# Re-timing the gates, input terms and early loads of a fused recurrence and feed-forward kernel

## The chip, the cores and the metric

The kernel runs on one core of one Trainium2 chip. The metric is device time in microseconds (us); lower is better. Kernels are compared only within the same rounds.

## The reference, cut to what matters

```python
# x, f_logit: (4, 6080, 256); lower_bound: (256,); w_in: (256, 2048); w_out: (2048, 256)
sig = 1 / (1 + exp(-f_logit))
f = lower_bound + (1 - lower_bound) * sig
for t in range(S):                       # a linear recurrence along the tokens
    h = f[:, t] * h + (1 - f[:, t]) * x[:, t]
    y[:, t] = h
h = y.reshape(24320, 256) @ w_in         # "first matmul"
out = (h * cos(h)) @ w_out               # "second matmul"
```

## The kernel before

Tokens go in chunks: seven of 256 (0 to 6), then chunks of 512 from chunk 7 on. For each chunk:

- a *gate* (tanh on ScalarE), *less-one* (tanh − 1), then the *terms* ih and u = (tanh − 1)·x;
- a transposition (by TensorE for chunks 0 to 3, by DMA later), the *forget gate* ff (GpSimd from chunk 4), two *scans* ya (VectorE, one for each half of the 256 features), and two *casts* yb to fp16 (GpSimd from chunk 4);
- then groups of the first matmul, a cosine (ScalarE), a product T (VectorE), and the second matmul.

The first matmul of a chunk needs both casts. In the traces here an engine takes its instructions in the order in which the program emits them, so the program weaves the preparation of later chunks between the groups of the current one. "(s, g)" is the place after group g of chunk s; "step s" is the stretch in which TensorE runs chunk s's first matmul.

```python
NPE, NSMALL = 4, 7
...
def less_one(c):                                   # ScalarE
    nc.scalar.activation(ig[:, ks, :], ig[:, ks, :], AFT.Identity, bias=-1.0, scale=1.0)

def pool_term(c):                                  # GpSimd: ih, then u
    nc.gpsimd.tensor_copy(by_half(ih), split(ig))
    for k in range(nt):
        nc.gpsimd.tensor_tensor(by_half(u)[:, k], split(ig)[:, k], split(xt)[:, k], AOP.mult)
...
def cast(c, i, a=0, b=None):
    ...
    eng = nc.vector if c < NPE else nc.gpsimd
    eng.tensor_scalar(yb[:, a:b], held[f"ya{i}", c][:, a:b], hc[:, i:i + 1], None, AOP.mult)
...
def front(c):
    gate(c); less_one(c); pool_term(c); turn(c)

FRONT = {NPE: (NPE - 2, 0), 5: (3, 0), 6: (3, 2), NSMALL: (4, 0), NSMALL + 1: (5, 0)}
for c in range(3, NC):
    ...
    elif c < NSMALL:
        at(c - 1, 0, forget(c)); at(c - 1, 0, recur(c, 0), cast(c, 0))
        at(c - 1, 1, recur(c, 1), cast(c, 1))
    elif c == NSMALL:
        at(c - 2, 3, forget(c))
        ...                                        # recur and cast as above
    if c >= NPE:
        if c in FRONT:
            at(*FRONT[c], front(c))
        else:
            at(c - 3, groups(c - 3) - 1, gate(c))
            at(c - 2, 0, less_one(c), pool_term(c), turn(c))
...
for s in range(2, NC):
    emit_load(s + 4)
    for g in range(groups(s)):
        moe1(s, g)                                 # first matmul, cosine, product
        moe2(*steps.pop(0))                        # a piece of the second matmul of chunk s - 1
        for what in weave.get((s, g), []):
            what()
```

(The `at` calls are shown without their lambdas.)

## Time and profile before

| | |
|---|---|
| time before | 694.66 us, median of 3 (693.38 to 694.71) |
| TensorE busy | 674.7 us of a span of 693.3 |
| TensorE idle before 90 us | 15.5 us |
| from the bulk start of chunk 8 (85.66 us) to the end | 607.6 us |

How to read it: TensorE is the engine that sets the time, so only its idle time and its clock matter. From 90 to 650 us it never pauses. What counts is at what moment the *bulk* of each early chunk's first matmul starts. One of its matmuls can begin with the first cast alone (a row "x1"); the rest, the bulk, needs the second. In the timeline the bulk is the row "x7" (chunks of 256) or "x3" (chunks of 512) that shows the wait; where there is no such wait, it is the row of the whole group, "x8" or "x4". The lines are in the prediction.

### The profile page before, as it was taken

Reading aid. Unit: us, or ns where it says so; the run is one execution under the profiler, and the core shown is the slowest. Engines: PE = TensorE matmul, PEld = TensorE weight load, DVE = VectorE, ACT = ScalarE, POOL = GpSimd, SP = SyncE. Lnnn points to the kernel's source line nnn. Section 1 sums busy time; section 2 is a strip of 40 time slices with the busy share of each in tenths; the row PEclk is TensorE's granted clock in tenths of the full one; section 3 lists DMA queues with packets and bytes.
Section 4 is the critical chain, followed back from the end, with each engine's and each line's share of the span. In section 5 each row is a group of like instructions: output and inputs, shape, how many; then the busy total and the mean of one; then the engine's idle time right before and its main releaser. Section 6 shows DMA issues by size and latency. Waiting matters only on the chain.

```text
span 693.3 us, 12206 instructions
## 1 busy us (share of the span) xinstructions
PE 674.7 (97%) x4726; PEld 484.8 (70%) x4726; DVE 583.9 (84%) x511; ACT 521.7 (75%) x593; POOL 390.8 (56%) x440
## 2 busy tenths in 40 slices
PE   6988899999999999999999999999999999999998
PEld 4787577777777777777777777777777777777776
DVE  5776878888888888888888888888888888888884
ACT  6685777778777877787778777877787778777763
POOL 3366656565656565656565656565556555655510
PEclk9999999999999999999999999999999999999999
DMA  9568557756864676468557765576457746662401
GB/s 230 157 179 209 144 126 180 145 122 164 177 147 122 161 183 142 122 156 187 145 122 156 185 146 122 158 184 146 122 154 180 153 122 153 184 151 62 92 31 61
DMA packets 172138, 101.99 MB, mean 147 GB/s; under 512 B 99120, under 2 KB 170544, under 8 KB 172080
## 3 DMA queue, kind: packets, MB, share of 16 engines
q1 hardware_dynamic: 170048, 97.54, 58.3%
q0 software_dynamic: 1760, 3.67, 2.2%
q8 instruction: 37, 0.61, 0.4%
q14 instruction: 21, 0.17, 0.1%
q10 hardware_dynamic: 272, 0.00, 0.0%
HBM read 54.00 MB, written 24.90 MB: 114 GB/s over the span
## 4 chain that ended last, share of the span: by engine, by line
PE 88%; DVE 3%; POOL 3%; ACT 2%; issue 2%; DMA 1%; SPq 0%; POOLq 0%; ACTq 0%
PE pb L286 44%; PE pa L250 44%; DVE T L265 2%; DMA xt<-in_x_dram 1%; DVE ya L214 1%; POOL u L158 1%; POOL yb L225 1%; ACT cs L259 1%; ACT ig L145 1%; POOL ih L156 0%; ACT ig L122 0%; SPq L82 0%; DVE u L138 0%; DVE yb L225 0%; ACT yb L221 0%
## 5 line engine op out<-in xcount | busy, mean ns | idle before, releaser
L265 DVE TENSOR_TENSOR T<-pa,cs 128x1024 f16<-128x1024 f32 x380 | 449.7, 1212 | 94.3 <-ACT cs L259 94.1
L259 ACT ACTIVATE cs<-pa 128x1024 f32<-128x1024 f32 x380 | 388.5, 1026 | 153.8 <-PE pa L250 149.2
L250 PE MATMUL pa<-yb,wi 128*128 128x512 f16 (+2 forms) x1640 | 393.2, 366 | 12.8 <-POOL yb L225 7.1
L286 PE MATMUL pb<-wo,T 128*128 128x256 f16 x3040 | 393.4, 273 | 0.0
L286 PEld LDWEIGHTS <-T 128*128 128x128 f16 x3040 | 297.7, 98 | 103.8 <-DVE T L265 0.3
L250 PEld LDWEIGHTS <-wi 128*128 128x128 f16 x1640 | 183.3, 114 | 94.1 <-issue 13.1
L225 POOL TENSOR_SCALAR yb<-ya,hc 128x512 f16<-128x512 f32 (+1 forms) x94 | 143.3, 1525 | 152.9 <-DVE ya L214 147.2
L214 DVE TENSOR_TENSOR_SCAN ya<-ff,ya,ut 128x512 f32<-128x512 f32 (+4 forms) x94 | 130.6, 1389 | 0.0
L158 POOL TENSOR_TENSOR u<-ig,xt 128x256 f16<-128x256 f32 x182 | 128.5, 739 | 0.0
L156 POOL CAST ih<-ig 128x1024 f16<-128x1024 f32 (+1 forms) x47 | 47.7, 1016 | 110.1 <-ACT ig L145 110.1
L195 POOL TENSOR_SCALAR ff<-it,hp 128x512 f32<-128x512 f16 (+1 forms) x94 | 63.0, 684 | 1.4 <-DMA it<-ih 1.4
L294 ACT COPY osb<-pb 128x512 f32<-128x512 f32 x93 | 53.9, 579 | 0.0
L122 ACT ACTIVATE ig<-zt 128x1024 f32<-128x1024 f32 (+2 forms) x52 | 51.5, 991 | 1.0 <-DMA zt<-in_f_logit_dram 0.9
L145 ACT ACTIVATE ig<-ig 128x1024 f32<-128x1024 f32 (+1 forms) x47 | 48.8, 1038 | 0.2
L310 PE MATMUL warm<-junk 128*128 128x512 f16 x14 | 6.0, 585 | 1.3 <-POOL junk L302 1.3
L138 DVE SCALAR_TENSOR_TENSOR u<-ig,xt 128x512 f16<-128x512 f32 (+1 forms) x5 | 2.9, 582 | 3.2 <-DMA xt<-in_x_dram 3.2
L214 DVE TENSOR_TENSOR_SCAN ya<-ff,ut 128x320 f32<-128x320 f32 (+2 forms) x6 | 5.6, 927 | 0.0
L214 DVE TENSOR_TENSOR_SCAN ya<-ff,ya,tp 128x256 f32<-128x256 f32 (+1 forms) x8 | 5.0, 665 | 0.6 <-ACT ff L192 0.4
L291 DVE COPY osb<-pb 128x256 f32<-128x256 f32 x4 | 1.7, 425 | 4.5 <-PE pb L286 4.5
L336 POOL COPY mark<-wo 128x1 f16<-128x1 f16 x1 | 0.2, 188 | 8.9 <-DMA wo<-in_moe_w_out_dram 8.9
L192 ACT ACTIVATE ff<-tp,hc 128x256 f32<-128x256 f16 (+1 forms) x10 | 3.7, 424 | 1.7 <-PE tp L172 1.6
L221 ACT ACTIVATE yb<-ya,hc 128x256 f16<-128x256 f32 (+1 forms) x5 | 2.3, 465 | 3.2 <-DVE ya L214 3.2
(27 smaller groups left out, 28.3 us busy)
## 6 DMA issues: line engine op xcount, KB each, us to landing
zt<-in_f_logit_dram SPq DMA_DIRECT2D x44, 512.0 KB, 5.1
xt<-in_x_dram SPq DMA_DIRECT2D x44, 512.0 KB, 6.2
out_dram<-osb SPq DMA_DIRECT2D x43, 512.0 KB, 3.4
out_dram<-osb SPq DMA_DIRECT2D x7, 256.0 KB, 2.6
wir<-in_moe_w_in_dram SPq DMA_DIRECT2D x2, 512.0 KB, 5.5
wo<-in_moe_w_out_dram POOLq DMA_DIRECT2D x4, 256.0 KB, 8.5
zt<-in_f_logit_dram POOLq DMA_DIRECT2D x4, 256.0 KB, 3.6
xt<-in_x_dram POOLq DMA_DIRECT2D x4, 256.0 KB, 3.7
```

Source lines behind the costliest of these rows:

```text
L122: nc.scalar.activation(ig[:, ks, :], zt[:, ks, :], AFT.Tanh, bias=0.0, scale=0.5)
L145: nc.scalar.activation(ig[:, ks, :], ig[:, ks, :], AFT.Identity, bias=-1.0, scale=1.0)
L156: nc.gpsimd.tensor_copy(by_half(ih), split(ig))
L158: nc.gpsimd.tensor_tensor(by_half(u)[:, k], split(ig)[:, k], split(xt)[:, k], AOP.mult)
L195: nc.gpsimd.tensor_scalar(f[:, a:b], igt[:, i, 0:b - a], hp[:, i:i + 1], 1.0, AOP.mult, AOP.add)
L214: nc.vector.tensor_tensor_scan(ya[:, p:q], f[:, p:q], ut[:, i, p - a:q - a], init, AOP.mult, AOP.add)
L225: eng.tensor_scalar(yb[:, a:b], held[f"ya{i}", c][:, a:b], hc[:, i:i + 1], None, AOP.mult)
L250: nc.tensor.matmul(pa[c, g][:, jq, a:b], win_block(i, jt), held[f"yb{i}", c][:, a:b], start=(i == 0), stop=(i == ND - 1))
L259: nc.scalar.activation(cs[c, g], pa[c, g], AFT.Sin, bias=float(_HALF_PI), scale=1.0)
L265: nc.vector.tensor_tensor(T, pa[c, g], cs[c, g], AOP.mult)
L286: nc.tensor.matmul(ps[:, ts % 2, :], Tt[c, jt][:, ts * P:(ts + 1) * P], wo[:, jt, :], start=(jt == 0), stop=(jt == NJ - 1))
L294: nc.scalar.copy(osb[:, ts - 1:ts + 1, :], ps)
```

## The change

Its intent: the gates and terms of each chunk are issued a step sooner, the early token loads move from GpSimd's to SyncE's queue, chunk 0's second matmul is woven with chunk 1's first, and chunks 2 and 3 get their terms from ScalarE and GpSimd instead of VectorE. No matmul is added or removed. The core of the diff (the bookkeeping of layouts for chunks 2 and 3, and lambdas rewritten as `later(...)`, are cut):

```diff
 def less_one(c):
-        nc.scalar.activation(ig[:, ks, :], ig[:, ks, :], AFT.Identity, bias=-1.0,
-                             scale=1.0)
+        if NPE <= c < NSMALL:
+            nc.gpsimd.tensor_scalar(ig[:, ks, :], ig[:, ks, :], -1.0, None, AOP.add)
+        else:
+            nc.scalar.activation(ig[:, ks, :], ig[:, ks, :], AFT.Identity, bias=-1.0,
+                                 scale=1.0)
 ...
-    load_wout(3)
-
-    mark2 = cpool.tile([P, 1], f16, name="mark2")
-    nc.gpsimd.tensor_copy(mark2, wo[:, NJ - 1, 0:1])
-    emit_load(3, q=nc.gpsimd)
+    w_in_place = load_wout(3)
+
+    for c in range(3, 7):
+        for k in emit_load(c):
+            if c == 3:
+                tc.add_manual_dep(k.ins, w_in_place.ins.name, ...)
 ...
+    gate(2)
+    less_one(2)
+    pool_term(2)
     moe1(1, 0)
-    moe1(1, 1)
-    gate(2)
-    term(2)
-    moe1(1, 2)
-    moe1(1, 3)
     moe2(0, 0)
+    mm1(1, 1)
+    cosine(1, 1)
+    moe2(0, 1)
     turn(2)
     forget(2)
     settle(2)
-    for h in range(1, 4):
-        moe2(0, h)
+    product(1, 1)
+    moe1(1, 2)
+    moe2(0, 2)
+    moe1(1, 3)
+    moe2(0, 3)
+    gate(3)
+    less_one(3)
+    pool_term(3)
 ...
-    FRONT = {NPE: (NPE - 2, 0), 5: (3, 0), 6: (3, 2), NSMALL: (4, 0), NSMALL + 1: (5, 0)}
+    FRONT = {NPE: ((2, 0), (2, 0)), NPE + 1: ((2, 2), (2, 3))}
 ...
+        if c == NPE:
+            f, slots = (c - 1, 1), ((c - 1, 1), (c - 1, 2))
 ...
+        first, second = FRONT.get(c, ((c - 3, groups(c - 3) - 1), (c - 2, 0)))
+        at(*first, later(gate, c))
+        at(*second, later(less_one, c), later(pool_term, c), later(turn, c))
 ...
-    for c in range(4, 6):
-        emit_load(c, q=nc.gpsimd)
-        if s + 4 < NC:
-            emit_load(s + 4)
+        if s + 5 < NC:
+            emit_load(s + 5)
```

More of the change, by code (lines that the diff above doesn't have):

```diff
@@ L105, in load_wout @@
     def load_wout(q):
-        nc.gpsimd.dma_start(
+        return nc.gpsimd.dma_start(
             wo[:, q * wc:(q + 1) * wc, :],
@@ L122, in gate @@
         nc.scalar.activation(ig[:, ks, :], zt[:, ks, :], AFT.Tanh, bias=0.0, scale=0.5)
-        if c >= NPE:
-            return
         if c == 0:
@@ L152, in pool_term @@
         u = hold("u", c, [P, CH // P, D], f16, 3)
-        by_half = lambda t: (t.rearrange("p k d -> p (k d)")[:, 0:nt * D]
-                             .rearrange("p (i k d) -> p k i d", i=ND, k=nt))
         split = lambda t: t[:, 0:nt, :].rearrange("p k (i d) -> p k i d", i=ND)
+        if c < NPE:
+            by_half = split
+        else:
+            by_half = lambda t: (t.rearrange("p k d -> p (k d)")[:, 0:nt * D]
+                                 .rearrange("p (i k d) -> p k i d", i=ND, k=nt))
         nc.gpsimd.tensor_copy(by_half(ih), split(ig))
@@ L163, in turn @@
         if c < NPE:
-            if c < 3:
-                d = ppool.tile([P, 2, ND, HALF], f16, tag="p2", bufs=2, name=f"tp{c}_{a}")
-            else:
-                d = ppool.tile([P, 2, ND, HALF], f16, tag="p1", bufs=3, name=f"tp{c}",
-                               padded_shape=[P, 2, ND, CH])
+            d = ppool.tile([P, 2, ND, HALF], f16, tag="p2", bufs=2, name=f"tp{c}_{a}")
             for q, src in enumerate((held["ih", c], held["u", c])):
@@ L192, in forget @@
                 nc.scalar.activation(f[:, a:b], igt[:, i, 0:b - a], AFT.Identity,
-                                     bias=1.0, scale=hc[:, i:i + 1])
+                                     bias=1.0, scale=(hc if c < 2 else hp)[:, i:i + 1])
             else:
@@ L332 @@
     load_wout(2)
-    load_wout(3)
-    mark2 = cpool.tile([P, 1], f16, name="mark2")
-    nc.gpsimd.tensor_copy(mark2, wo[:, NJ - 1, 0:1])
-    emit_load(3, q=nc.gpsimd)
+    w_in_place = load_wout(3)
+    for c in range(3, 7):
+        for k in emit_load(c):
+            if c == 3:
+                tc.add_manual_dep(k.ins, w_in_place.ins.name, mybir.DependencyInfo(
+                    mybir.DependencyClass.Sync, mybir.DependencyReason.DATA))
     keep_warm(7)
@@ L382, with later @@
     settle(2)
-    for h in range(1, 4):
-        moe2(0, h)
-    def front(c):
-        gate(c)
-        less_one(c)
-        pool_term(c)
-        turn(c)
+    product(1, 1)
[6 more added lines that the diff above has]
+    pool_term(3)
     weave = {}
-    FRONT = {NPE: (NPE - 2, 0), 5: (3, 0), 6: (3, 2), NSMALL: (4, 0), NSMALL + 1: (5, 0)}
+    FRONT = {NPE: ((2, 0), (2, 0)), NPE + 1: ((2, 2), (2, 3))}
     def at(s, g, *what):
         weave.setdefault((s, g), []).extend(what)
+    def later(f, *args):
+        return lambda: f(*args)
@@ L400 @@
     for c in range(3, NC):
         if c < NPE:
-            at(c - 1, 0, lambda c=c: gate(c), lambda c=c: term(c))
-            at(c - 1, 1, lambda c=c: turn(c), lambda c=c: forget(c), lambda c=c: settle(c))
+            at(c - 1, 1, later(turn, c), later(forget, c), later(settle, c))
+            continue
+        if c == NPE:
+            f, slots = (c - 1, 1), ((c - 1, 1), (c - 1, 2))
         elif c < NSMALL:
-            at(c - 1, 0, lambda c=c: forget(c))
-            at(c - 1, 0, lambda c=c: recur(c, 0), lambda c=c: cast(c, 0))
@@ L407 @@
-            at(c - 1, 1, lambda c=c: recur(c, 1), lambda c=c: cast(c, 1))
+            f, slots = (c - 1, 0), ((c - 1, 0), (c - 1, 1))
         elif c == NSMALL:
-            at(c - 2, 3, lambda c=c: forget(c))
-            at(c - 1, 0, lambda c=c: recur(c, 0), lambda c=c: cast(c, 0))
-            at(c - 1, 1, lambda c=c: recur(c, 1), lambda c=c: cast(c, 1))
-        else:
-            at(c - 1, 0, lambda c=c: forget(c))
-            at(c - 1, 2, lambda c=c: recur(c, 0), lambda c=c: cast(c, 0))
-            at(c - 1, 4, lambda c=c: recur(c, 1), lambda c=c: cast(c, 1))
@@ L416 @@
-        if c >= NPE:
-            if c in FRONT:
-                s, g = FRONT[c]
-                at(s, g, lambda c=c: front(c))
-            else:
-                at(c - 3, groups(c - 3) - 1, lambda c=c: gate(c))
-                at(c - 2, 0, lambda c=c: less_one(c), lambda c=c: pool_term(c),
-                   lambda c=c: turn(c))
+            f, slots = (c - 2, 3), ((c - 1, 0), (c - 1, 1))
+        else:
+            f, slots = (c - 1, 0), ((c - 1, 2), (c - 1, 4))
+        at(*f, later(forget, c))
@@ L425 @@
+        for i, slot in enumerate(slots):
+            at(*slot, later(recur, c, i), later(cast, c, i))
+        first, second = FRONT.get(c, ((c - 3, groups(c - 3) - 1), (c - 2, 0)))
+        at(*first, later(gate, c))
+        at(*second, later(less_one, c), later(pool_term, c), later(turn, c))
     steps = [(c, h) for c in range(1, NC) for h in range(2 * chunks[c][1] // P)]
-    for c in range(4, 6):
-        emit_load(c, q=nc.gpsimd)
     for s in range(2, NC):
-        if s + 4 < NC:
-            emit_load(s + 4)
+        if s + 5 < NC:
+            emit_load(s + 5)
```

## The prediction

> **What bounds the kernel now.** I read the page first (busy shares, slices), then the busy table by stretch, then the waits of TensorE, then the timelines of TensorE and GpSimd over the first 90 us. The page and the busy table:
>
> ```profile
> PE 674.7 (97%) x4726; PEld 484.8 (70%) x4726; DVE 583.9 (84%) x511; ACT 521.7 (75%) x593; POOL 390.8 (56%) x440
> ```
> ```profile
> 50.00:60.00 10.00, 7.09 (x50) 5.69 (x49) 5.88 (x7) 5.56 (x6) 6.80 (x10) 0.83 1.15 276
> ...
> 90.00:100.00 10.00, 10.00 (x72) 7.12 (x70) 9.09 (x9) 6.92 (x8) 6.80 (x8) 1.00 0.39 54
> ...
> 300.00:400.00 100.00, 100.00 (x695) 71.00 (x694) 87.65 (x75) 78.12 (x87) 59.41 (x66) 1.00 0.68 154
> ```
>
> Columns after the stretch are its length, busy us of PE, PEld, DVE, ACT, POOL, then granted clock. From 90 to 650 us TensorE never stops, at full clock, and the change neither adds nor removes a matmul. So 600 of the 693 us can't move. The movable part is before 90 us: summing length less PE busy over its nine stretches gives 15.5 us idle (2.3 of it before any data exists), plus stretches at a granted clock of 0.5. The waits of TensorE name two causes:
>
> ```profile
> PE pa L250 <- POOL yb L225: 7.1, 5, 2.9
> PE pa L250 <- DVE T L265: 4.0, 3, 2.2
> ```
>
> The five waits for yb are one at the start of each of chunks 4 to 8. The longest, chunk 5, in TensorE's and then GpSimd's timeline (start, length):
>
> ```profile
> 50.80 0.27 PE L250 MATMUL pa<-yb,wi 128*128 128x256 f16 x1
> 53.99 0.92 PE L250 MATMUL pa<-yb,wi 128*128 128x256 f16 x7 [2.91 <-POOL yb L225]
> 54.75 1.85 PE L286 MATMUL pb<-wo,T 128*128 128x256 f16 x8
> ```
> ```profile
> 48.00 0.93 POOL L225 TENSOR_SCALAR yb<-ya,hc 128x256 f16<-128x256 f32 x1 [1.26 <-ACT ig L145]
> 48.87 1.04 POOL L156 CAST ih<-ig 128x1024 f16<-128x1024 f32 x1
> 49.88 3.15 POOL L158 TENSOR_TENSOR u<-ig,xt 128x256 f16<-128x256 f32 x4
> 53.02 0.92 POOL L225 TENSOR_SCALAR yb<-ya,hc 128x256 f16<-128x256 f32 x1
> ...
> 68.74 1.57 POOL L225 TENSOR_SCALAR yb<-ya,hc 128x512 f16<-128x512 f32 x1 [3.32 <-DVE ya L214]
> 71.05 1.56 POOL L225 TENSOR_SCALAR yb<-ya,hc 128x512 f16<-128x512 f32 x1 [0.74 <-DVE ya L214]
> ```
>
> GpSimd casts the first half of chunk 5's scan, then works 4.2 us on a later chunk's cast and input term (ih, u of chunk 7), and only then casts the second half, whose scan had ended at 51.15. TensorE has one matmul to do and waits. After it, eight matmuls take 1.85 us instead of 1.04: half clock. The last two lines are chunk 7: nothing stands between its two casts, and TensorE waits only 1.28 us.
>
> **What the Trainium skill says.** "Perfetto Trace Analysis", section on the tensor engine instruction: VectorE, ScalarE and GpSimd take instructions strictly in order. The trace agrees: the cast ready at 51.15 starts at 53.02, when u ends. So the order of GpSimd's queue decides, not its 56% share. "TensorE: Matmul & The Clock Gate", Part 1: an idle window of about 3.4 us (free-running) halves the clock, and a busy window restores it. Here the clock is 0.50 from about 17.4 to 20.7 us and 54.9 to 58.3 us, each after an idle of 2.2 and 2.9 us; both begin on one grid of 3.41 us (11 windows apart). Each costs about 1.7 us. Idles of 1.3 us brought none. "GPSIMD Engine Reference", 3.1: about 2.6 cycles an element for two inputs, 512 elements of one input at best 769 ns. Here u of 256 elements takes 739 ns, the forget gate of 512 697 ns, but the yb cast of 512 1566 ns: dearer than the page's best.
>
> **The change part by part.**
>
> *Early loads on SyncE.* Six load issues of GpSimd (0.73 us each, 4.4 us at 19.84 to 24.27) and an 8.9 us wait for w_out leave its queue. GpSimd did nothing useful then (next work at 31.10), and no load wait of consequence stands in the first 90 us behind chunk 1. Worth 0 by itself; it makes room for chunk 2's and 3's terms.
>
> *Chunks 2 and 3.* Their ih and u leave VectorE (0.42 + 0.68 us each), which is the limit from 12.3 to 27 us, and go to ScalarE (0.63) and GpSimd (0.6 + 1.4). Chunk 0's second matmul is woven with chunk 1's first. The 2.19 us wait at 16.84 and the dip after it stay, since everything before is unchanged. From there TensorE has, until chunk 2's first matmul, 8 groups of 0.87 us, 0.7 of transposes and 1.7 of dip: 26.2 at the earliest, against 26.80 (bulk 27.29). Chunk 3's start comes out at about 34.1 against 35.31. Gain 1.1 us.
>
> *Chunk 4.* Its two scans move one group later (behind products 1 and 2 of chunk 3 instead of 0 and 1). Group 2's matmul begins 3.5 us into the step, its product ends about 3.5 later, the scan takes 0.8 and the cast 0.92: 8.7 us, or more as ScalarE is late there by about 1 us for gates 4 and 5, against a step of 7.0. I make it 9.4: chunk 4's bulk at 43.5 against 43.93. Most of the 1.1 is given back. But here ih and u of chunk 5 no longer stand between the casts.
>
> *Chunks 5 to 8: GpSimd's order.* The build's order of both kernels shows what stands between a chunk's two casts:
> chunk 4: before ih, u of 5; after nothing.
> chunk 5: before ih, u of 7; after less-one, ih, u of 6.
> chunk 6: before ih, u of 8; after ih, u of 7.
> chunk 7: before nothing; after ih, u of 8 (512 tokens).
> The "sooner" is not so for 7 and 8: the step that ran them in one go at steps 4 and 5 is gone, and they come a step later. Now each interval from bulk start to bulk start, as a chain: first product ends +3.25 (43.93 to 47.17); scan 0.74; to GpSimd 0.17; cast, insert, cast.
> Step 4: 4.16 + 0.92 + insert + 0.92. Insert: less-one about 1.0 (estimate, between 0.7 and 1.57 of like rows) + 0.61 + 1.42 = 3.0. Sum 9.0; before 10.06 (43.93 to 53.99).
> Step 5: insert 1.04 + 2.9 to 3.2: sum 10.1; before 10.14.
> Step 6 (casts of 512): 3.25 + 1.27 + 0.17 + 1.57 + (1.04 + 2.85) + 1.57 = 11.7; before 8.54 (64.13 to 72.67).
> From 43.5: 52.5, 62.6, 74.3, against 72.67. So chunk 7 starts 1.6 us later than before. TensorE has then been idle for about 11.7 - 6.9 = 4.8 us, less any dip in step 6, so step 7 begins at half clock: 1.7 to 2.1 us, of which about half hides the 2.0 us of waits that step 7 has anyway (81.6 and 85.0). About 1 us more. The dip at 55 us disappears, but it was hidden: chunk 6 waited on GpSimd's chain, not on TensorE.
>
> Sum: -0.4 to chunk 4, -1.1 in step 4, 0 in step 5, +3.2 in step 6, +1.0 in step 7: +2.7, rounded down a little for what I may have missed in chunks 1 to 3. From 694.66: 697.0. After chunk 8, TensorE is full in both.
>
> **The rivals.** (1) The start gains more: if chunks 1 to 3 run without VectorE as limit and the dip at 17.4 vanishes, and TensorE fills every hole, the most to be had is 11.1 us of yb and T waits and some 2 of the 3.4 us of dips: 682. For it: those are the waits aimed at. Against: the waits move with GpSimd's order, and step 6 is worse by 3 us in any case. A middle of this, 690, is what it takes if ScalarE is not late in steps 2 and 3 and less-one is cheap. (2) GpSimd becomes the limit of the whole of steps 4 to 7: less-one at 1.57 us or dips in steps 4, 6 and 7 would give 700. For: idles of 2 to 5 us. (3) The loads are hidden anyway and all is a wash: 694 to 695.
>
> **Range and chances.** 2% is 13.9 us, more than all removable waits together, and no loss I can find exceeds 6. So within 2% is nearly sure: 0.97; faster 0.02, slower 0.01. The 8-in-10 range is the sum with -4.5 (half of rival 1) and +3.5 (rival 2): 692.5 to 700.5.
>
> **What would show it.** In the changed profile: six load issues gone from GpSimd; chunk 2's bulk near 26.2 and chunk 4's near 43.5; in GpSimd's timeline less-one, ih, u between the casts of chunk 5 and ih, u between those of chunk 7; the wait of chunk 7's first matmul for yb 3 to 5 us instead of 1.28, and half clock after it; less-one near 1.0 us. It is wrong if chunk 7 starts before 72.7, if the clock stays full through 90 us, or if chunk 2 starts before 25.

## The result, and the profile after

The changed kernel took 697.39 us (median of 4, 697.27 to 697.71), the kernel before in the same rounds 694.52 us. The ratio is 1.0045, 95% interval 1.0028 to 1.0063: slower by about 0.4%, well within 2%.

The page and the busy table of the changed kernel (length, then busy us of PE, PEld, DVE, ACT, POOL, granted clock, DMA share, GB/s):

```profile
PE 673.9 (97%) x4726; PEld 484.4 (70%) x4726; DVE 582.8 (84%) x507; ACT 520.7 (75%) x592; POOL 393.5 (57%) x442
```
```profile
60.00:70.00 10.00, 8.65 (x64) 7.29 (x64) 5.96 (x6) 5.08 (x6) 5.96 (x7) 0.83 0.53 159
70.00:80.00 10.00, 5.91 (x28) 3.51 (x28) 3.04 (x4) 5.02 (x6) 8.12 (x11) 0.83 0.69 197
...
90.00:100.00 10.00, 10.00 (x71) 7.08 (x70) 8.90 (x8) 7.04 (x9) 5.75 (x7) 1.00 0.60 120
```

TensorE's work is the same and it is full from 90 to 650 us, as before. The new hole is at 70 to 80 us: 5.91 us of matmuls, a lowered clock, and GpSimd the busiest engine. The waits of TensorE:

```profile
PE pa L250 <- POOL yb L225: 11.0, 5, 4.1
PE pa L250 <- DVE T L265: 2.4, 4, 0.7
```

Waits for VectorE's products fell from 4.0 to 2.4 us, those for GpSimd's casts rose from 7.1 to 11.0. Where they are, in TensorE's timeline:

```profile
48.69 0.27 PE L250 MATMUL pa<-yb,wi 128*128 128x256 f16 x1
51.29 0.93 PE L250 MATMUL pa<-yb,wi 128*128 128x256 f16 x7 [2.33 <-POOL yb L225]
...
61.35 1.65 PE L250 MATMUL pa<-yb,wi 128*128 128x256 f16 x7 [2.92 <-POOL yb L225]
...
69.62 0.38 PE L250 MATMUL pa<-yb,wi 128*128 128x512 f16 x1
74.09 1.09 PE L250 MATMUL pa<-yb,wi 128*128 128x512 f16 x3 [4.09 <-POOL yb L225]
74.98 1.91 PE L286 MATMUL pb<-wo,T 128*128 128x256 f16 x8
```

Chunk 5 waits 2.33 us (2.91 before), chunk 6 2.92 (1.33), chunk 7 4.09 (1.28). After the wait of 2.92 us the next seven matmuls take 1.65 us instead of 0.93, and after the one of 4.09 us a row of eight takes 1.91 instead of 1.04: half clock. GpSimd's timeline shows what stands between the casts of chunk 5 and of chunk 7:

```profile
45.88 0.92 POOL L225 TENSOR_SCALAR yb<-ya,hc 128x256 f16<-128x256 f32 x1 [3.21 <-DVE ya L214]
46.78 1.50 POOL L144 TENSOR_SCALAR ig<-ig 128x512 f32<-128x512 f32 x1
48.34 0.61 POOL L160 CAST ih<-ig 128x512 f16<-128x512 f32 x1
48.91 1.42 POOL L162 TENSOR_TENSOR u<-ig,xt 128x256 f16<-128x256 f32 x2
50.30 0.93 POOL L225 TENSOR_SCALAR yb<-ya,hc 128x256 f16<-128x256 f32 x1
...
66.68 1.56 POOL L225 TENSOR_SCALAR yb<-ya,hc 128x512 f16<-128x512 f32 x1 [4.04 <-DVE ya L214]
68.19 1.57 POOL L160 CAST ih<-ig 128x1024 f16<-128x1024 f32 x1
69.73 2.77 POOL L162 TENSOR_TENSOR u<-ig,xt 128x256 f16<-128x256 f32 x4
72.48 1.55 POOL L225 TENSOR_SCALAR yb<-ya,hc 128x512 f16<-128x512 f32 x1
```

Both lie as the build's order had shown: less-one, ih and u of chunk 6 inside chunk 5's pair, ih and u of chunk 8 inside chunk 7's. Note the bracket of the first line of each pair: GpSimd had idled 3 to 4 us for the scan just before. The work was put on the wrong side of the first cast.

The bulk starts, read from each kernel's timeline of TensorE (us), for all kernels:

| kernel | chunk 4 | 5 | 6 | 7 | 8 |
|---|---|---|---|---|---|
| before | 43.93 | 53.99 | 64.13 | 72.67 | 85.66 |
| changed | 41.81 | 51.29 | 61.35 | 74.09 | 88.17 |
| changed, second trace | 41.99 | 51.47 | 61.54 | 73.44 | 87.28 |
| e1 terms of 8 early | 42.13 | 51.61 | 61.68 | 71.68 | 84.66 |
| e2 terms of 6, 7 early | 41.79 | 48.67 | 57.05 | 68.96 | 82.76 |
| e3 terms of 6, 7, 8 early | 41.89 | 48.77 | 57.15 | 67.16 | 80.14 |
| e4 less-one on ScalarE | 42.70 | 50.97 | 61.03 | 73.43 | 88.27 |
| e6 new start, old places | 42.21 | 52.27 | 62.34 | 70.87 | 83.85 |
| e7 old start, new places | 42.99 | 52.48 | 62.92 | 74.83 | 89.83 |
| e8 before, loads on SyncE | 42.40 | 52.46 | 62.53 | 72.89 | 86.12 |
| e9 changed, loads on GpSimd | 50.86 | 60.34 | 70.98 | 82.90 | 97.61 |
| e10 e3 and casts on ScalarE | 40.80 | 47.68 | 56.12 | 64.32 | 77.58 |
| e11 changed, clock kept full | 41.26 | 50.74 | 60.83 | 72.76 | 85.74 |

From chunk 8's start to the end of the span it is 607.6 us in the kernel before (693.3 − 85.66), 607.7 in the changed one (695.9 − 88.17), in e9 (705.3 − 97.61) and in e10 (685.3 − 77.58). So everything is decided before chunk 8, and a difference in that column is the difference of the spans.

### The profile page after: what moved, and what is told of

Its sections match the earlier page's. It is cut to its first block, busy times and chain, and to the rows that moved or that the text cites. A ratio compares the mean times of both kernels' runs of the same rounds, so it can differ in the third digit from the quotient of the medians.

```text
span 695.9 us, 12212 instructions
## 1 busy us (share of the span) xinstructions
PE 673.9 (97%) x4726; PEld 484.4 (70%) x4726; DVE 582.8 (84%) x507; ACT 520.7 (75%) x592; POOL 393.5 (57%) x442
## 4 chain that ended last, share of the span: by engine, by line
PE 88%; POOL 3%; DVE 3%; DMA 2%; issue 2%; ACT 2%; SPq 0%; POOLq 0%; ACTq 0%
PE pb L286 45%; PE pa L250 44%; DMA wo<-in_moe_w_out_dram 1%; DVE ya L214 1%; ACT cs L259 1%; DVE T L265 1%; POOL yb L225 1%; POOL u L162 1%; DMA xt<-in_x_dram 1%; POOL ih L160 0%; POOL wo L106 0%; POOL wi L93 0%; POOL ig L144 0%; SPq L82 0%; ACT osb L294 0%
## 5 line engine op out<-in xcount | busy, mean ns | idle before, releaser
L162 POOL TENSOR_TENSOR u<-ig,xt 128x256 f16<-128x256 f32 x186 | 130.5, 731 | 0.0
L160 POOL CAST ih<-ig 128x1024 f16<-128x1024 f32 (+1 forms) x49 | 49.2, 1003 | 117.9 <-ACT ig L146 117.8
L144 POOL TENSOR_SCALAR ig<-ig 128x512 f32<-128x512 f32 x3 | 4.5, 1501 | 0.7 <-ACT ig L122 0.7
L136 DVE SCALAR_TENSOR_TENSOR u<-ig,xt 128x256 f16<-128x256 f32 (+1 forms) x3 | 1.5, 511 | 3.6 <-DMA xt<-in_x_dram 3.6
L310 PEld LDWEIGHTS <-junk 128*128 128x128 f16 x14 | 1.6, 124 | 3.0 <-issue 1.4
```

## The experiments

Theory A: the order of GpSimd's queue between the casts of a chunk sets the next start. Theory B: the loss comes from another part (less-one on GpSimd, the new start, the loads), and the places are neutral. There are eleven runs, all correct. Ratios are against the kernel before in the same rounds (5 rounds each).

**e1: terms of chunk 8 alone.**

```diff
-    FRONT = {NPE: ((2, 0), (2, 0)), NPE + 1: ((2, 2), (2, 3))}
+    FRONT = {NPE: ((2, 0), (2, 0)), NPE + 1: ((2, 2), (2, 3)), 8: ((5, 2), (5, 3))}
```

> Changed kernel with one edit: gate, less-one and input terms of chunk 8 go back one step, to the end of step 5, ahead of chunk 7's first cast instead of between chunk 7's two casts. Theory A (GpSimd's order between a chunk's casts sets the start of the next chunk): the interval from chunk 6's to chunk 7's bulk start falls from 12.7 us to about 8.5, the half clock in step 7 goes, total about 5 us less than the changed kernel, 692 us, so below the kernel before. Theory B (the loss comes from less-one on GpSimd or from the early loads, the order is incidental): within 0.5 us of the changed kernel, 697.

Measured: 694.26 us, ratio 0.9998 (0.9979 to 1.0017), against 1.0045 for the changed kernel: one edit takes the whole loss back. (The edit moves chunk 8's gate and transposition along with the terms.) Theory A holds, but the size was off: 3.1 us instead of 5 (against the changed kernel's 697.39 us, which is of other rounds). Step 6 took 10.0 us (61.68 to 71.68), not 8.5. GpSimd's timeline of e1 says why:

```profile
61.60 1.36 POOL L195 TENSOR_SCALAR ff<-it,hp 128x512 f32<-128x512 f16 x2
62.91 1.04 POOL L160 CAST ih<-ig 128x1024 f16<-128x1024 f32 x1
63.91 3.73 POOL L162 TENSOR_TENSOR u<-ig,xt 128x256 f16<-128x256 f32 x4
67.61 4.01 POOL L225 TENSOR_SCALAR yb<-ya,hc 128x512 f16<-128x512 f32 x2
```

There is no gap from 61.6 to 71.6: now GpSimd's work itself is the limit of this step. It is also dearer than I had counted: u takes 3.73 us for four instead of 2.77, the casts 4.01 for two instead of 3.11. A likely reason shows in e3 below.

**e2: terms of chunks 6 and 7, with the forget gates of 5 and 6.**

```diff
+    FRONT = {..., 6: ((3, 2), (3, 3)), 7: ((4, 2), (4, 3))}
         elif c < NSMALL:
-            f, slots = (c - 1, 0), ((c - 1, 0), (c - 1, 1))
+            f, slots = (c - 2, 2), ((c - 1, 0), (c - 1, 1))
```

> Changed kernel with the terms of chunks 6 and 7, and the forget gates of 5 and 6, moved to the end of the step before, ahead of the first casts of chunks 5 and 6; chunk 8 stays between chunk 7's casts. Theory A: the intervals of steps 4 and 5 fall from 9.5 and 10.1 us to about 7.1 each (TensorE's own work), while step 6 keeps its 11.7 to 12.7; total about 5 to 6 us less than the changed kernel, 691 to 692 us, with the 4 us wait at chunk 7 still there. Theory B: about 697.

Measured: 693.17 us, ratio 0.9982 (0.9962 to 1.0002). Step 4 is 6.9 us, with no wait left. Step 5 is 8.4, as chunk 7's less-one on ScalarE comes late (GpSimd waits 0.82 us for it) and u is slow here too (3.18 us for four instead of 2.77). Step 6 is 11.9, with its wait of 4.65 us. The gain is 4.2 us of the expected 5 to 6.

**e3: both moves.**

> Both moves together: no other chunk's terms stand between two casts of any chunk. Theory A: steps 4 and 5 at about 7.1 us, step 6 at about 8.5 (three instructions of GpSimd chained behind one scan), no half clock after 40 us; total about 10 us less than the changed kernel, 687 us, some 7 below the kernel before. If the gains do not add (GpSimd simply has too much work in steps 4 to 6), about 690 to 692.

Measured: 690.24 us, ratio 0.9938 (0.9920 to 0.9955). The gains of e1 and e2 add (3.1 + 4.2 = 7.3, measured 7.2 below the changed kernel), but they fall short of the 10 expected, by the same 1.5 us in step 6 and 1.3 in step 5. The clock stayed full from 12 to 96 us in its trace. The view of the casts between 62 and 76 us (minimum, median, maximum), and the VectorE row of the time:

```profile
L225 POOL TENSOR_SCALAR yb<-ya,hc x3: 1559/1562/2477, 63.1 to 75.1; 128x512 f16<-128x512 f32 x3
```
```profile
62.93 1.27 DVE L214 TENSOR_TENSOR_SCAN ya<-ff,ya,ut 128x512 f32<-128x512 f32 x1
```

The cast that begins at 63.09 while this scan runs takes 2.48 us instead of 1.56: it overlaps the scan for 1.11 us and loses 0.92. The Trainium skill has this in "SBUF — State Buffer", section "SBUF: two separate sides": a VectorE instruction with two SBUF inputs and a GpSimd instruction that reads SBUF exclude each other. The scan reads ff and ut, both in SBUF. In the changed kernel ih at 68.19 is slow too: 1.57 us instead of 1.04, beside a scan from 67.66 to 68.93. But the trace agrees only in part: the cast at 66.68 (1.56 us) overlaps that same scan by 0.58 us, and neither takes longer than alone (1.56 and 1.27). So that the two exclude each other is an inference from some of the overlaps and the page, and not shown; no run here took the scan away.

**e4: less-one of chunks 4 to 6 on ScalarE again.**

```diff
-        if NPE <= c < NSMALL:
+        if False:
             nc.gpsimd.tensor_scalar(ig[:, ks, :], ig[:, ks, :], -1.0, None, AOP.add)
```

> Changed kernel with less-one of chunks 4 to 6 on ScalarE again, as it was before the change. Theory A: only chunk 6's less-one lies in a chain that counts (1.5 us between the casts of chunk 5), so chunk 5 starts about 1.5 us earlier and nothing else changes: 695.9 us, 1.5 below the changed kernel. Theory B (less-one on GpSimd is the loss): 3 us or more below, back to 694.5.

Measured: 697.94 us, ratio 1.0046 (1.0030 to 1.0063): the same as the changed kernel. Theory B with less-one as the loss falls. But my expectation missed as well. Step 4 is 1.2 us shorter (8.27 against 9.48), as foreseen. Chunk 4 starts 0.9 us later, and TensorE waits 0.70 us longer for it: in ScalarE's queue two less-ones (0.63 and 0.65 us, at 28.48 and 35.18) stand among the cosines of chunks 2 and 3. In its trace half clocks lengthen step 6 to 12.40 us and step 7 to 14.84, against 11.90 and 13.84 in the second trace of the changed kernel.

**e6 and e7: the other two corners.** e6 has the changed start and loads with the old places; e7 the old start and loads with the new places and less-one on GpSimd.

```diff
 # e6, on the changed kernel (and less-one on ScalarE as in e4)
+    FRONT = {NPE: ((2, 0), (2, 0)), 5: ((3, 0), (3, 0)), 6: ((3, 2), (3, 2)),
+             NSMALL: ((4, 0), (4, 0)), NSMALL + 1: ((5, 0), (5, 0))}
-        if c == NPE:
-            f, slots = (c - 1, 1), ((c - 1, 1), (c - 1, 2))
-        elif c < NSMALL:
+        if c < NSMALL:
 # e7, on the kernel before: less_one() and the whole weave of the changed kernel
```

> Changed kernel's start and early loads (chunks 0 to 3), but the places of gates, terms, forget gates and scans of chunks 4 to 8 as in the kernel before, less-one on ScalarE. Theory A (the start gains about 2 us, the places in steps 4 to 7 lose about 5): chunk 4 starts near 42, chunk 7 some 28.7 us later, total 2 us below the kernel before: 692.4. Theory B (the new start costs, the places are neutral): at or above 694.5, near the changed kernel.

> The opposite corner: kernel before with its own start and loads, but the changed places for chunks 4 to 8 and less-one of 4 to 6 on GpSimd. Theory A: chunk 4 starts near 44, chunk 7 some 32 us later, then half clock in step 7: 4 to 5 us above the kernel before, 699. Theory B: about 694.5.

Measured: e6 693.88 us, ratio 0.9987 (0.9975 to 0.9998); e7 699.25 us, ratio 1.0058 (1.0046 to 1.0070). In thousandths of the time before:

| | old places | new places |
|---|---|---|
| old start and loads | 0 | +5.8 |
| new start and loads | −1.3 | +4.5 |

The new places (with less-one on GpSimd) cost 5.8 thousandths, 4.0 us, with either start. The new start gains 1.3 thousandths, 0.9 us, with either set of places. Within the intervals (4.6 to 7.0 for e7, −2.5 to −0.2 for e6, 2.8 to 6.3 for the changed kernel, which its second run puts at +3.9) the two add. Theory A holds; the start is worth half of what e6 was expected to show, and is barely clear of zero.

**e8: the early loads alone, on the kernel before.**

```diff
-    load_wout(3)
-    mark2 = ...; nc.gpsimd.tensor_copy(mark2, wo[:, NJ - 1, 0:1]); emit_load(3, q=nc.gpsimd)
+    w_in_place = load_wout(3)
+    for c in range(3, 7): ...            # on SyncE's queue, as in the change; s + 5 in the loop
```

> Kernel before with only the early token loads changed (chunks 3 to 6 on SyncE's queue, no wait of GpSimd for w_out, one more chunk ahead). The prediction gave this part 0 by itself: 694.5, within 0.5 us of the kernel before. Rival: the earlier loads take bandwidth from w_out or let chunk 4 start earlier, 1 us or more either way.

Measured: 695.11 us, ratio 0.9996 (0.9982 to 1.0009): nothing, as predicted.

**e9: the changed kernel with the loads back on GpSimd.**

```diff
-    for c in range(3, 7): ...
+    mark2 = cpool.tile([P, 1], f16, name="mark2")
+    nc.gpsimd.tensor_copy(mark2, wo[:, NJ - 1, 0:1])
+    for c in range(3, 6):
+        emit_load(c, q=nc.gpsimd)
+    emit_load(6)
```

> Changed kernel, but token loads of chunks 3 to 5 issued by GpSimd after it has waited for w_out, as before the change. GpSimd's queue then holds that wait and six issues (4.4 us, ending near 24.3 us) ahead of chunk 2's terms, which ran at 18.8 us. If the early loads are what lets the terms of chunk 2 go to GpSimd: chunk 2's first matmul moves from 25.5 to about 29.5 us and the total rises by about 4 us, to 701. If the place of the loads is of no account here too: 697.4.

Measured: 707.05 us, ratio 1.0175 (1.0154 to 1.0196): 9.4 us above the changed kernel in the same rounds, over twice what I expected. GpSimd's and TensorE's timelines of e9:

```profile
21.60 0.19 POOL L336 COPY mark<-wo 128x1 f16<-128x1 f16 x1 [10.92 <-DMA wo<-in_moe_w_out_dram]
...
26.16 0.63 POOL L160 CAST ih<-ig 128x512 f16<-128x512 f32 x1
```
```profile
26.85 0.61 PE L172 MATMUL tp<-ident,ih 128*128 128x128 f16 x4 [4.67 <-POOL ih L160]
```

The terms of chunk 2 ran at 26.16 instead of 18.80 us (w_out landed 2 us late here, on top of the six issues). TensorE idled 4.67 us and then ran at half clock from 27 to 33 us, and chunk 4 started 8.9 us later than in the second trace of the changed kernel. So the part that is worth nothing alone is indispensable beside the new start.

**after_again: the changed kernel once more.**

> The changed kernel itself, unaltered, on the same chip as the two runs beside it: 697.4 us, and a second trace that shows whether the half clock after 61 us and the absence of one before 21 us repeat. Waits of chunks 5 to 7 for GpSimd's casts should repeat within 0.2 us, half clocks need not.

Measured: 697.69 us, ratio 1.0039 (1.0022 to 1.0056). Only one of the three waits repeats within 0.2 us: chunk 5's, 2.32 us (2.33). Chunk 6's is 1.26 (2.92) and chunk 7's 4.66 (4.09), because half clocks, which do not repeat, make TensorE itself slower and so shorten its waits. In the first trace they ran from 61 to 64 and 74.5 to 78 us, in this one from 52 to 56 and 73 to 76. What GpSimd sets repeats better: chunk 6 starts 10.07 us after chunk 5 (10.06), while chunk 7 starts 11.90 us after chunk 6, against 12.74 in the first trace, where a half clock lay in step 6.

**e11: spare matmuls in the two longest waits.**

```diff
+        if s == 5:
+            keep_warm(12)
+        if s == 6:
+            keep_warm(18)
```

> Changed kernel with 12 and 18 spare matmuls of 512 columns put on TensorE where it waits for chunk 6 and for chunk 7, so that its clock stays full; they take 2.6 and 3.9 us of waits of 2.9 and 4.1 to 4.7 us. The prediction put the half clock of step 7 at about 1 us on the path and any half clock of step 6 at nothing, as GpSimd sets chunk 7's start. If so: chunk 7 starts as in the changed kernel, chunk 8 follows 13.0 us later instead of 14.1, total 1.1 us lower, 696.3. If half clocks cost their whole 1.7 us each: 3 us lower, 694. If they cost nothing: 697.4.

Measured: 696.25 us, ratio 1.0015 (1.0000 to 1.0030), 1.4 us below the changed kernel in the same rounds. The clock was full from 8 to 94 us. TensorE's timeline of e11:

```profile
67.70 4.05 PE L310 MATMUL warm<-junk 128*128 128x512 f16 x18
72.76 0.81 PE L250 MATMUL pa<-yb,wi 128*128 128x512 f16 x3 [0.79 <-POOL yb L225]
```

The spare matmuls fill the wait and chunk 7 does not come later: 11.9 us after chunk 6, as in the second trace. Step 7 takes 12.98 us instead of 14.08 and 13.84. The half clock after chunk 7 starts costs about 1 us (0.7 us of the difference between these two traces lies before chunk 4). One in step 5 costs little: with the new places step 5 is 10.07 to 10.64 us in the traces that have one there (after_again, e1, e7, e9), 10.06 to 10.09 in those that don't (changed, e4, e11). But one in step 6 is not free, as the expectation had it: 12.74 against 11.90 us in the two traces of the changed kernel, 10.36 (e8) against 8.53 (e6) with the old places.

**e10: a version that beats both.** e3, with the second casts of chunks 4, 6 and 7 on ScalarE, after the last cosine of the step.

```diff
-        if c < NPE and i == 0:
+        if c < NPE and i == 0 or c in (4, 6, 7) and i == 1:
 ...
-            at(*slot, later(recur, c, i), later(cast, c, i))
+            at(*slot, later(recur, c, i))
+            at(*((c - 1, 3) if c in (4, 6, 7) and i == 1 else slot), later(cast, c, i))
```

> Terms of 6, 7 and 8 early as in e3, and the second casts of chunks 4, 6 and 7 on ScalarE, placed after its last cosine of the step. In e3 GpSimd was busy without a pause from chunk 6's casts to chunk 7's (10.0 us). If its work is the limit there, step 6 falls to about 7.8 us and chunks 4 and 6 start 0.4 to 0.6 us earlier: some 3 us below e3, 687. If ScalarE, waiting in order for the scans, delays the cosines instead, no better than e3, 690.

Measured: 687.41 us, ratio 0.9893 (0.9880 to 0.9906): 1.1% below the kernel before, and the best. Step 6 is 8.2 us, chunk 4 starts at 40.80. The waits of TensorE in e10:

```profile
PE pa L250 <- DVE T L265: 3.6, 4, 1.3
...
PE pa L250 <- POOL yb L225: 1.7, 3, 1.2
```

GpSimd's casts cost 1.7 us instead of 11.0, and those now on ScalarE another 1.7. The largest wait left is for VectorE's products, around chunks 1 and 7. Step 6 and chunk 4's wait (0.98 us instead of 1.50) gained, as expected; step 5 did not (8.44 us against 8.38 in e3). Some of chunk 4's earlier start is chance: chunk 2 starts at 25.07 against 25.66 in e3, before any of the edits acts.

## Why the prediction was right, point by point

- *The total.* 697.0 was predicted, 697.39 and 697.69 measured. The sign and the mechanism hold: e1 to e3 remove the loss by moving the groups that the prediction named (with their gates and transpositions and, in e2 and e3, the forget gates of chunks 5 and 6).
- *Chunk 4's start, "-0.4".* This is the term that was mis-sized. The pair of traces shows −2.1 (43.93 to 41.81), the two-by-two table −0.9 us for the start as a whole. The step that failed reads "The 2.19 us wait at 16.84 and the dip after it stay, since everything before is unchanged." The instructions were unchanged, but neither the wait nor the half clock was bound to them. The wait for chunk 0's products was 0.65 and 1.56 us in the two traces of the changed kernel; in the others it ran from 0.39 (e8, old start) to 2.18 (e6, new start). It is 2.1 to 2.2 us only where TensorE had not waited for w_in just before (before, e6, e11); in the first changed trace such waits, of 0.24 and 0.95 us, came ahead of it. The half clock at 17 us is missing in both traces of the changed kernel, and also in e7 and e8, which keep the old start; e9, with the new start, has one at 16 to 20 us. The trace of the kernel before happened to have one, which makes the start's gain look twice as large. "I make it 9.4" for step 3 was too high as well: 8.8 in the trace (33.01 to 41.81), as ScalarE seems to have been less late (argued, not tested).
- *Step 4, "-1.1".* Measured −0.6 (9.48 against 10.06). Less-one took 1.50 us, not the 1.0 that I had estimated; the group row of the changed kernel:

```profile
L144 POOL TENSOR_SCALAR ig<-ig 128x512 f32<-128x512 f32 x3 | 4.5, 1501 | 0.7 <-ACT ig L122 0.7
```

- *Step 5, 0.* 10.06 against 10.14. Right.
- *Step 6, "+3.2" from a step of 11.7.* The second trace and e11 give 11.9, the first trace 12.7: there a half clock delayed the first product by 0.7 us (it begins 2.75 us after the bulk start instead of 2.02 in the second). Beside a scan ih took 1.46 to 1.57 us instead of 1.04 in all three. Right, with a half clock that was not in the sum.
- *Step 7, "+1.0".* 14.08 and 13.84 against 12.99; e11 shows that keeping the clock full brings it back to 12.98. Right.
- *The loads, 0 by themselves, and room for the terms.* e8 and e9 bear both out, e9 with more force than I expected.
- *Rivals.* The gain of rival 1 was there in small (0.9 us). Rival 2's further half clocks came in some executions and not in others. Rival 3 is out: the interval excludes 1.

In the pair of traces the terms −2.1, −0.6, −0.1, +4.2, +1.1 sum to +2.5 us, the difference of chunk 8's starts. The total came out so near partly by luck: the start gained more and step 6 lost more than I had said.

Why does a wait of a given length bring a half clock in one execution and not in another? The traces answer most of it. Within a trace the half clocks start whole multiples of 3.41 us apart: 37.54 us in the kernel before (11), 13.66 in the changed kernel (4), 20.48 in its second trace (6). So a grid of windows of 3.41 us can be laid over each of the ten traces that have a half clock, and the idle time of TensorE counted in each window between 5 and 96 us:

| trace, wait that ends at | idle us, by window | half clock after it |
|---|---|---|
| changed, 51.29 | 1.62 + 0.70 | no |
| second trace, 51.47 | 2.32 in one | at 52.5 |
| changed, 61.35 | 2.38 + 0.53 | at 60.8 |
| e6, 62.34 | 1.66 + 1.26 | no |
| e8, 52.46 | 1.91 + 1.00 | no |

The windows just before 17 of the 18 half clocks hold 2.02 to 3.41 us of idle time; no window at full clock without a half clock after it holds more than 1.91. The one exception is e6, with 1.76 us before a half clock at 9.9. A half clock lasted one window, or two where TensorE idled 0.79 us or more within the first. So the length of a wait and how it falls on the grid decide together, and the grid lies differently in each execution: which start gets a half clock is luck.

Open: whether the border between 1.91 and 2.02 us holds elsewhere, and how much of the slow u and casts in e1 and e3 is the scan.

## What to carry to other kernels

Where an engine takes instructions strictly in order, look at what stands between an instruction that becomes ready and the one before it; "issued sooner" is a gain only if the work lands in a gap of that queue and not in front of the instruction on which the busiest engine waits. GpSimd was busy for 57% of the time and still set four starts; moving three groups from behind the first cast to the idle time ahead of it was worth 7 us, a hundredth of the kernel. Test parts of a re-timing in pairs: the loads were worth 0 alone and 9 us beside the new start.

## What the Trainium skill lacked or had wrong

- "TensorE: Matmul & The Clock Gate", Part 1, gives an idle window of about 3.4 us, free-running, as the condition for half clock. The grid agrees (starts 4, 6 and 11 windows of 3.41 us apart), but a window need not be wholly idle: 2.02 us of idle time in one was enough (e9, at 16.2 us), while 1.91 (e8, from 48.0 us) brought none. The page does not say how little work in a window is enough.
- "GPSIMD Engine Reference", 3.1, gives 769 ns as the best case for 512 elements. Here two operations on 512 elements beat it: the forget gate (float16 to float32, two operations) took 692 ns and a cast from float32 to float16 610 ns. A plain float32 to float32 add of a constant took 1501 ns and a multiplication from float32 to float16 1563 ns. The section's only time for a whole instruction of a named operation is one float32 add of two tensors; it has none by type.
- "SBUF — State Buffer", section "SBUF: two separate sides", is borne out only in part: a cast of 1.56 us took 2.48 beside a scan of 1.27 (e3), but in the changed kernel such a cast and scan overlapped by 0.58 us and took 1.56 and 1.27, as alone. The page does not name the scan among the instructions with two SBUF inputs.
